# Last transform stage of three batches split into even and odd rows, with sums and differences of index pairs made beforehand

## Chip, cores and metric

One core of one Trainium2 chip. The metric is the device time of one execution in microseconds, the median of several; all runs told of here are fast, with a granted TensorE clock of 0.995 or more. PE is TensorE (PEld its weight loads), DVE VectorE, ACT ScalarE, POOL GpSimd, SP the engine that only issues transfers. A record is one instruction in a trace.

## The reference, cut to what matters

```python
# x, v: (4, 12544, 128)
u = x * v
y = irfft(rfft(u, n=2*S, axis=1) * rfft(h_filt, n=2*S, axis=0)[None], n=2*S, axis=1)[:, :S]   # long convolution
a = (x * y).reshape(4 * 12544, 128)
h = maximum(maximum(a @ w1, a @ w2), a @ w3)                     # 128 -> 768
out = h @ w_out                                                  # 768 -> 128
```

The kernel makes the convolution as a transform of length 128 x 90 with matmuls. The last stage of the inverse goes over 90 indices k1 to 98 rows n: y[n] = sum over k1 of z[k1] * e(n (k1 + 1/4) / 90), real part. Everything is fp32.

## The kernel before

Four batches. Batch 0 is transformed first. Then each of 32 tiles a batch goes through the last transform (`t_last`) and six slots (f = 0 to 5) of the feed-forward part (`up`, `down`), and beside batch b's tiles, slot by slot, the convolution of batch b + 1 runs (`conv_steps`): first its forward part (the u steps), then 45 pairs of k1 (the g steps).

```python
def halves_mm(out, lhsT, rhs, start, stop):        # two 64-column halves, side by side in the array
    for h in range(2):
        nc.tensor.matmul(out[64*h:64*h+64], lhsT[:, 64*h:64*h+64], rhs, ...)

def g_third(b, g):                                  # third transform of a pair of k1, result to DRAM
    ...                                             # 8 matmuls into PSUM ps
    zs = cv.tile([P, 2, 256], tag="z", bufs=2)
    nc.scalar.copy(zs, ps)                          # ACT
    nc.scalar.dma_start(zd[b][2*g:2*g+2], zs)       # issued by ACT

def t_last(i):                                      # last transform of one tile
    for s in range(4):
        for c in range(2):                          # real, imaginary part
            halves_mm(ps[:, s*NB:(s+1)*NB], zt[:, c, s*D:(s+1)*D], f4[:, c, :], ...)   # NB = 98
    nc.vector.tensor_tensor(out=g, in0=ps, in1=xT, op=mult)

def up(i, f):                                       # hps: two PSUM buffers, one for pa, one for pb
    halves_mm(pa, w_sb[1][:, f*P:(f+1)*P], g);  nc.scalar.activation(h, pa, Relu)         # ACT
    halves_mm(pb, w_sb[2][:, f*P:(f+1)*P], g);  nc.vector.tensor_tensor(h, h, pb, max)    # DVE

for f in range(NF):                                 # one slot
    h = up((b, i), f)
    down(*late)                                     # of the slot before
    if f == 3: t_last(tiles[n + 1])
    run(beside.pop(s, ()))                          # this slot's convolution steps
```

`pa` of a slot needs the buffer that ACT's relu of the slot before frees, `pb` the one that DVE's maximum frees. In the views `ops` is the PSUM buffer of `down`, `hid` what relu and maximum write, `eo`, `xt`, `xs` and `ab` are tiles of the g steps, and the first matmuls of the filter's transform (`ps<-f1h`) are called the first quad.

## Time and profile before

| | before |
|---|---|
| time | 2530.8 us (2528.8 to 2533.3) |
| start of the first last transform | 320.7 us |
| batch 0's tiles (batch 1's transform beside) | 581.3 us |
| batch 1's, batch 2's tiles | 586.2, 586.2 us |
| batch 3's tiles (nothing beside) | 452.9 us |
| PE busy | 99% |

The stages run from the first matmul into tile yps of a batch to that of the next (or to the end). The lines that carry the argument are in the prediction.

### The profile page before, as it was taken

The numbers are of one execution on the slowest core, as the hardware profiler recorded it, in microseconds if no ns is written. First come the engines' busy times: TensorE is split into PE (matmuls) and PEld (weight loads), VectorE is DVE, ScalarE is ACT, GpSimd is POOL, SyncE is SP. The second block draws the span as 40 slices with busy tenths as digits, with TensorE's granted clock in tenths as the row PEclk, the third lists the DMA queues.
The fourth block names the chain that finished last, engine by engine and source line by source line (L and its number), as shares of the span: only waits on it lengthen the run. The fifth ranks groups of instructions, "written<-read, shape, count | busy, mean of one in ns | idle before, by whom it ended". The sixth has DMA issues, their size and how long they took to land. (4 is left out here: it accounts for less than half of the span.)

```text
span 2527.3 us, 62508 instructions
## 1 busy us (share of the span) xinstructions
PE 2491.1 (99%) x26393; PEld 1512.2 (60%) x26393; DVE 1259.7 (50%) x2494; ACT 1042.2 (41%) x1980; POOL 57.5 (2%) x112
## 2 busy tenths in 40 slices
PE   8999999999999999999999999999999999999999
PEld 7888755655556556656566556555666654444444
DVE  5588733356666633336666633335667642222222
ACT  2688823344444423334444433333544432222222
POOL 1022200000000000000000000000000000000000
PEclk9999999999999999999999999999999999999999
DMA  7789754477877544466888834447888842222221
GB/s 165 172 251 279 234 122 95 101 179 202 222 208 208 159 104 102 89 143 180 229 222 236 218 91 97 101 105 181 222 234 219 233 112 54 58 59 53 59 53 35
DMA packets 429070, 384.51 MB, mean 152 GB/s; under 512 B 291454, under 2 KB 338293, under 8 KB 428789
## 3 DMA queue, kind: packets, MB, share of 16 engines
q1 hardware_dynamic: 305840, 291.63, 46.1%
q10 hardware_dynamic: 117893, 74.73, 10.3%
q0 software_dynamic: 5056, 14.16, 1.9%
q8 instruction: 206, 3.38, 0.6%
q14 instruction: 75, 0.61, 0.1%
HBM read 295.73 MB, written 84.67 MB: 151 GB/s over the span
## 5 line engine op out<-in xcount | busy, mean ns | idle before, releaser
L473 DVE TENSOR_TENSOR hid<-hid,pb 128x392 f32<-128x392 f32 x768 | 431.8, 562 | 777.6 <-PE pb L126 672.8
L470 ACT ACTIVATE hid<-pa 128x392 f32<-128x392 f32 x768 | 382.2, 498 | 725.2 <-PE pa L126 657.8
L126 PE MATMUL pa<-gt,w_sb 128*64 128x392 f32 x3072 | 640.3, 495 | 11.4 <-ACT hid L470 10.7
L126 PE MATMUL pb<-gt,w_sb 128*64 128x392 f32 x3072 | 636.4, 493 | 4.9 <-DVE hid L473 4.3
L126 PE MATMUL ops<-hid,wo_sb 128*64 128x392 f32 x3072 | 635.8, 492 | 0.1
L126 PEld LDWEIGHTS pb<-gt,w_sb 128*64 128x64 f32 x3072 | 216.6, 136 | 297.4 <-issue 202.4
L126 PEld LDWEIGHTS ops<-hid,wo_sb 128*64 128x64 f32 x3072 | 219.9, 137 | 286.0 <-issue 285.3
L126 PEld LDWEIGHTS pa<-gt,w_sb 128*64 128x64 f32 x3072 | 192.8, 137 | 151.2 <-issue 105.6
L135 PEld LDWEIGHTS ps<-f,uT 98*64 98x64 f32 x4096 | 183.4, 138 | 59.9 <-issue 57.2
L126 PEld LDWEIGHTS yps<-f,zt 90*64 90x64 f32 x4096 | 188.6, 136 | 47.2 <-issue 44.6
L378 DVE TENSOR_TENSOR xt<-xt,ht 128x512 f32<-128x512 f32 x180 | 124.5, 692 | 179.6 <-ACT xs L373 149.4
L126 PEld LDWEIGHTS ps<-ab,wt 128*64 128x64 f32 x2880 | 166.5, 137 | 51.8 <-issue 33.2
L135 PE MATMUL ps<-f,uT 98*64 98x90 f32 x4096 | 195.2, 243 | 1.4 <-issue 1.4
L126 PE MATMUL yps<-f,zt 90*64 90x98 f32 x4096 | 195.3, 247 | 0.0
L401 ACT COPY zs<-ps 128x512 f32<-128x512 f32 x180 | 105.6, 587 | 217.1 <-PE ps L126 211.9
L126 PE MATMUL ps<-ab,wt 128*64 128x128 f32 x2880 | 189.6, 274 | 0.6 <-DVE ab L389 0.6
L126 PE MATMUL ps<-spec,wt 128*64 128x128 f32 x2880 | 187.9, 273 | 0.0
L126 PEld LDWEIGHTS ps<-spec,wt 128*64 128x64 f32 x2880 | 164.6, 137 | 14.9 <-issue 14.7
L461 DVE TENSOR_TENSOR gt<-yps,xT 128x392 f32<-128x392 f32 x128 | 72.5, 567 | 161.0 <-PE yps L126 132.7
L372 ACT ACTIVATE xs<-xt 64x512 f32<-64x512 f32 x180 | 113.1, 628 | 77.4 <-DVE xt L152 46.1
L139 ACT COPY spec<-ps 128x360 f32<-128x360 f32 (+1 forms) x132 | 71.4, 544 | 167.1 <-PE ps L135 167.0
L389 DVE TENSOR_TENSOR ab<-xt 128x256 f32<-128x256 f32 x360 | 136.0, 419 | 1.6
(67 smaller groups left out, 1572.6 us busy)
## 6 DMA issues: line engine op xcount, KB each, us to landing
wt<-wt_const SPq DMA_DIRECT2D x135, 512.0 KB, 4.5
ht<-hd SPq DMA_DIRECT2D x270, 256.0 KB, 5.7
zd<-zs ACTq DMA_DIRECT2D x180, 256.0 KB, 4.8
zt<-zd SPq DMA_DIRECT2D x128, 360.0 KB, 5.7
ut<-in_xr_dram SPq DMA_DIRECT2D x128, 196.0 KB, 3.7
ut<-in_vr_dram SPq DMA_DIRECT2D x128, 196.0 KB, 4.1
xT<-in_x_dram SPq DMA_DIRECT2D x512, 49.0 KB, 4.1
out_dram<-ot ACTq DMA_DIRECT2D x128, 196.0 KB, 3.8
```

The costliest lines, as they stand in the source:

```text
L126: nc.tensor.matmul(out[64 * h:64 * h + 64], lhsT[:, 64 * h:64 * h + 64], rhs, start=start, stop=stop, skip_group_check=True)
L135: nc.tensor.matmul(ps[64 * c:64 * c + 64, 256 * i + r * N1:256 * i + (r + 1) * N1], a[:, r, :], table[:, c * N1:(c + 1) * N1], start=(i % ...
L139: copy(dst, ps[:].rearrange("p (s m) -> p s m", m=256)[:, :, 0:2 * N1].rearrange("p s (r k) -> p k r s", r=2))
L372: nc.scalar.mul(xs[0:64], xt[64:128], -1.0)
L378: nc.vector.tensor_tensor(out=xt[:], in0=xt[:], in1=hts[g][:, 0], op=ALU.mult)
L389: nc.vector.tensor_tensor(out=ab[:, :, q, :], in0=y[:, :, 0, :], in1=y[:, :, 1, :], op=op)
L401: nc.scalar.copy(zs[:].rearrange("p k f -> p (k f)"), ps[:])
L461: nc.vector.tensor_tensor(out=g[:], in0=ps[:, 0:N], in1=xTs.pop(i)[:].rearrange("d p n -> d (p n)"), op=ALU.mult)
L470: nc.scalar.activation(h[:], pa[:, 0:N], Relu)
L473: nc.vector.tensor_tensor(out=h[:], in0=h[:], in1=pb[:, 0:N], op=ALU.max)
```

## The change

For k1 and k1 + 45 the factor e(n k1 / 90) differs by (-1)^n. So even rows n need only sums z[k1] + z[k1 + 45], odd rows only differences. If sums and differences are made before, one pass over 45 real and 45 imaginary parts (again 90 rows of the array) yields the 49 even rows, a second one the 49 odd rows: half the moving columns. The sums are made in `g_third`, as the pair (k1, k1 + 45) is now one step g. The prologue and the folding of the weights were rearranged in the same change.

```diff
-    k1, n = np.arange(N1), np.arange(NB)
+    k1 = np.arange(N1).reshape(2, N1 // 2).T.ravel()      # 0, 45, 1, 46, ...
+    f4p = f4[::2].transpose(1, 0, 2).reshape(N1, NB // 2, 2).transpose(0, 2, 1)
 ...
 def g_third(b, g):
-        nc.scalar.copy(zs[:].rearrange("p k f -> p (k f)"), ps[:])
+        if b == 0:
+            nc.scalar.copy(zs[:].rearrange("p k f -> p (k f)"), ps[:])
+        else:
+            z1 = state["cv"][0].tile([P, 256], FP32, tag="z1", name="z1", bufs=2)
+            nc.scalar.copy(z1[:], ps[:, 256:512])
+            for a, op in enumerate((ALU.add, ALU.subtract)):
+                nc.vector.tensor_tensor(out=zs[:, a], in0=ps[:, 0:256], in1=z1[:], op=op)
         nc.scalar.dma_start(zd[b][2 * g:2 * g + 2]..., zs[:])
 ...
 def t_last(i):                      # batches 1 to 3
+            for s in range(4):
+                for a in range(2):
+                    halves_mm(y[:, s, a * h:a * h + h], zt[:, a, s * D:(s + 1) * D],
+                              f4p[:, a, :], s == 0 and a == 0, True)          # h = 49
 ...
 # prologue: win, eye, back loaded by GpSimd, not ACT
-    warm_up()                        # 16 rounds
+    warm_up(12)
+    window_back()                    # was after the second step of the filter
+    warm_up(20)
 ...
 # folding of the weights: the transpose one step ahead of the product
-    for f in range(NF):
-        folded = fold(f)
-        ...
-        folded()
+    folded = [fold(0)]
+    ...
+    for f in range(1, NF):
+        folded.append(fold(f))
+        folded.pop(0)()
+    folded.pop()()
```

Cut from the diff: two transfers for zt in place of one, the strided view of y, and `signs()`, split off from `window_back`.

More of the change, by code (lines that the diff above doesn't have):

```diff
@@ L40, in tables @@
     S = P * N1
-    k1, n = np.arange(N1), np.arange(NB)
+    k1 = np.arange(N1).reshape(2, N1 // 2).T.ravel()
+    n = np.arange(NB)
     a = e(np.outer(n, k1 + 0.25) / N1)
@@ L62, in tables @@
     f32 = np.float32
-    return f1.astype(f32), f1h.astype(f32), f4.astype(f32), np.ascontiguousarray(both, f32)
+    return f1.astype(f32), f1h.astype(f32), f4.astype(f32), f4p.astype(f32), np.ascontiguousarray(both, f32)
 @with_exitstack
@@ L98 @@
     zd = [dram.tile([N1, 2, 64, 256], FP32, name=f"zd{b}") for b in range(B)]
-    f1_t, f1h_t, f4_t, w_t = tables(NB)
+    f1_t, f1h_t, f4_t, f4p_t, w_t = tables(NB)
     f1_d = nc.inline_tensor(f1_t, name="f1_const").ap()
@@ L103 @@
     f4_d = nc.inline_tensor(f4_t, name="f4_const").ap()
+    f4p_d = nc.inline_tensor(np.ascontiguousarray(f4p_t), name="f4p_const").ap()
     wt_d = nc.inline_tensor(w_t, name="wt_const").ap()
@@ L249 @@
     for h in range(2):
+        nc.gpsimd.dma_start(
+            win[64 * h:64 * h + HH],
+            window[0, h * HH * P:(h + 1) * HH * P].rearrange("(n p) -> n p", p=P))
+    nc.gpsimd.dma_start(eye[:], eye_d)
+    nc.gpsimd.dma_start(back[:].rearrange("p r t -> p (r t)"), back_d)
+    for h in range(2):
         nc.scalar.dma_start(w1_sb[64 * h:64 * h + 64], w1[:, :])
@@ L256 @@
                 posT[:, (h * HH + lo_) * P:(h * HH + hi_) * P])
-    for h in range(2):
-        nc.scalar.dma_start(
-            win[64 * h:64 * h + HH],
-            window[0, h * HH * P:(h + 1) * HH * P].rearrange("(n p) -> n p", p=P))
-    nc.scalar.dma_start(eye[:], eye_d)
-    nc.scalar.dma_start(back[:].rearrange("p r t -> p (r t)"), back_d)
     nc.scalar.dma_start(f1h[:], f1h_d)
@@ L267, with warm_up @@
     nc.scalar.dma_start(f4[:], f4_d)
-    def warm_up():
+    def warm_up(n):
         ps = fps.tile([P, 1024], FP32, tag="cv", name="pw", bufs=2)
-        for _ in range(16):
+        for _ in range(n):
             halves_mm(ps[:, 0:256], warm[:, 0:P], warm[:], True, True)
@@ L281, in window_back, with signs @@
         nc.scalar.copy(winr[:].rearrange("n r t -> n (r t)"), pw[0:64 + HH, 512:512 + P])
+    def signs():
         for sg, lo_, m in ((0, 0, 1.0), (0, FO, 1.0), (1, 0, -1.0), (1, FO, 1.0)):
@@ L444, in t_load @@
         zt = hp.tile([N1, 2, 512], FP32, tag="zt", name="zt", bufs=2)
-        nc.sync.dma_start(
-            zt[:], zd[b][:, :, 2 * i:2 * i + 2, :].rearrange("k c t f -> k c (t f)"))
+        if b == 0:
+            nc.sync.dma_start(
+                zt[:], zd[b][:, :, 2 * i:2 * i + 2, :].rearrange("k c t f -> k c (t f)"))
+        else:
+            for c in range(2):
+                nc.sync.dma_start(
+                    zt[NK * c:NK * c + NK],
+                    zd[b].rearrange("(g a) c t f -> g a c t f", a=2)[
+                        :, :, c, 2 * i:2 * i + 2, :].rearrange("g a t f -> g a (t f)"))
         zts[b, i] = zt
@@ L455, in t_last @@
         ps = yps.tile([D, 512], FP32, tag="y", name="yps")
-        for s in range(4):
-            for c in range(2):
-                halves_mm(ps[:, s * NB:(s + 1) * NB], zt[:, c, s * D:(s + 1) * D],
-                          f4[:, c, :], s == 0 and c == 0, c == 1)
-        g = hp.tile([D, N], FP32, tag="g", name="gt", bufs=2)
-        nc.vector.tensor_tensor(out=g[:], in0=ps[:, 0:N],
-                                in1=xTs.pop(i)[:].rearrange("d p n -> d (p n)"), op=ALU.mult)
+        g = hp.tile([D, 4, NB], FP32, tag="g", name="gt", bufs=2)
+        y = ps[:, 0:N].rearrange("d (p n) -> d p n", p=4)
+        if i[0] == 0:
+            for s in range(4):
+                for c in range(2):
+                    halves_mm(y[:, s, :], zt[:, c, s * D:(s + 1) * D], f4[:, c, :],
+                              s == 0 and c == 0, c == 1)
+        else:
+            h = NB // 2
+            for s in range(4):
+                for a in range(2):
+                    halves_mm(y[:, s, a * h:a * h + h], zt[:, a, s * D:(s + 1) * D],
+                              f4p[:, a, :], s == 0 and a == 0, True)
+            y = y.rearrange("d p (a m) -> d p m a", a=2)
+        xT = xTs.pop(i)
+        if i[0] == 0:
+            nc.vector.tensor_tensor(out=g[:], in0=y, in1=xT[:], op=ALU.mult)
+        else:
+            nc.vector.tensor_tensor(out=g[:].rearrange("d p (m a) -> d p m a", a=2), in0=y,
+                                    in1=xT[:].rearrange("d p (m a) -> d p m a", a=2),
+                                    op=ALU.mult)
         gs[i] = g
     def up(i, f):
-        rhs = gs[i][:]
+        rhs = gs[i][:].rearrange("d p n -> d (p n)")
         h = hp.tile([P, N], FP32, tag="hid", name="hid")
@@ L478, in down @@
             pos_[i] = ops.tile([D, 512], FP32, tag="ops", name="ops")
-            halves_mm(pos_[i][:, 0:N], lin[:], gs[i][:], True, False)
+            halves_mm(pos_[i][:, 0:N], lin[:], gs[i][:].rearrange("d p n -> d (p n)"), True,
+                      False)
         halves_mm(pos_[i][:, 0:N], wo_sb[:, f, :], h[:], False, f == NF - 1)
@@ L534 @@
             mlp_in(i)
-        if i == 1:
-            window_back()
         if i:
             mlp_out(i - 1)
+    signs()
     mps.close()
@@ L658 @@
                 u_first(2 * (s - NK) + v // 2, v % 2, nc.scalar.copy)
-    for f in range(NF):
-        folded = fold(f)
-        if f == 0:
-            u_turn(4)
-            u_turn(5)
-        folded()
+    folded = [fold(0)]
+    u_turn(4)
+    u_turn(5)
+    for f in range(1, NF):
+        folded.append(fold(f))
+        folded.pop(0)()
+    folded.pop()()
     nc.scalar.copy(lin[:], pl[:, 0:D])
@@ L672 @@
     hp = ctx.enter_context(tc.tile_pool(name="hp", bufs=3))
+    f4p = hp.tile([N1, 2, NB // 2], FP32, name="f4p", bufs=1)
+    nc.scalar.dma_start(f4p[:], f4p_d)
     op_ = ctx.enter_context(tc.tile_pool(name="op", bufs=2))
```

## The prediction

> **What bounds the kernel now.** I read the page first (busy shares), then the groups by line, the chain of waits in time, the timeline of one tile, and last the PE waits and the first 60 us.
>
> ```profile
> PE 2491.1 (99%) x26393; PEld 1512.2 (60%) x26393; DVE 1259.7 (50%) x2494; ACT 1042.2 (41%) x1980; POOL 57.5 (2%) x112
> ...
> L126 PE MATMUL yps<-f,zt 90*64 90x98 f32 x4096 | 195.3, 247 | 0.0
> ...
> L401 ACT COPY zs<-ps 128x512 f32<-128x512 f32 x180 | 105.6, 587 | 217.1 <-PE ps L126 211.9
> ```
>
> PE is busy 99% of the span; DVE and ACT have half of it free. The last transform (tile yps) is 4096 records over 128 tiles, 32 a tile. A record's mean of 247 ns is mostly latency, so the cost of a tile is read from start to start, in the chain of waits in order of time (start, length, what) late in batch 3:
>
> ```profile
> 2130.03 1.36 PE yps L126 x32
> 2131.39 0.66 PE pa L126 x4
> 2132.05 0.66 PE pb L126 x4
> ```
>
> One tile's last transform holds PE for 1.36 us (16 pairs of records: two 64-column halves side by side), and the next work starts at once: no wait at either end. A dense group is 4 records (2 pairs) in 0.66 us. So a pair of 98 columns takes 1.355/16 = 84.7 ns (1.355 from the timeline below), a pair of 392 columns 329 ns: near 2 x columns / 2.4 GHz plus 2 to 3 ns (81.7 and 326.7 without the addition). Here the moving columns set the pace. The timeline shows what the weight loads do meanwhile:
>
> ```profile
> 2407.20 1.53 PE L126 MATMUL yps<-f,zt 90*64 90x98 f32 x32
> 2407.20 1.33 PEld L126 LDWEIGHTS yps<-f,zt 90*64 90x64 f32 x30 [0.18 <-issue]
> 2408.47 0.23 PEld L126 LDWEIGHTS pa<-gt,w_sb 128*64 128x64 f32 x4
> 2408.55 0.83 PE L126 MATMUL pa<-gt,w_sb 128*64 128x392 f32 x4
> ```
>
> Each record has its own weight load, which runs under the matmul before it. How long a load holds its path is seen where PE had stood still and two loads follow each other:
>
> ```profile
> 22.92 0.26 PEld L279 LDWEIGHTS pw<-back,winT 128*105 128x105 f32 x2 [0.51 <-ACT winT L278]
> ...
> 707.29 0.20 PEld L126 LDWEIGHTS pa<-gt,w_sb 128*64 128x64 f32 x4 [1.05 <-ACT hid L470]
> ```
>
> In the second line two pairs of 64-column loads end after 0.197 us while one load lasts 0.136: the second pair began about 0.055 us after the first (single records of the trace: 707.287 and 707.342). In the first, 105 columns: 0.26 - 0.17 = 0.09 us. That is 0.86 ns a column, and 54 to 55 ns for 64.
>
> **What the Trainium skill says.** (1) "TensorE: Matmul & The Clock Gate", section "LDWEIGHTS (loading the stationary operand)": a load takes its columns / 1.2 GHz, whatever the rows: 53.3 ns for 64. The trace agrees (55 ns, 90 ns for 105). (2) The same page, "Back-to-back issue gap": in a stream of loads and matmuls the spacing is set by both, and tiny matmuls have a floor of about 25 ns each. With two records side by side that floor would be 50 ns a pair, close to the load's 55; no run here reaches below it. (3) "TensorEngine Tiling (Array Packing)", "Key Properties": different tiles of the array load and multiply in parallel. The trace agrees: the halves start 6 to 8 ns apart. (4) The first page's Part 1 on the clock gate: half clock after an idle window, full clock after some 3.4 us of work. The trace agrees: see the first 23 us below.
>
> **The change part by part.**
>
> *Last transform, 96 of 128 tiles.* The count of matmuls and loads stays (4 positions x 2 x 2 halves); each now moves 49 columns in place of 98. By columns alone a pair would need 2 x 49 / 2.4 + 2 = 43 ns. But each pair still has a 64-column load, 54 to 55 ns, which starts only when the matmul before has begun (about 2 ns after, in the trace). So the load sets the pace: 56.5 ns. Saved per tile: 16 x (84.7 - 56.5) = 451 ns. All of it is on the path, as PE is the bound: 96 x 0.451 = **43.3 us**. So the columns halve, the time falls by a third.
>
> *Sums and differences of k1 and k1 + 45.* In 135 steps (3 x 45) the copy of 128x512 on ACT (587 ns) becomes a copy of 128x256 (373 ns, as the eo copies of the same shape): ACT loses 135 x 0.214 = 29 us. DVE gains 270 operations of the butterfly's form (128x256, one operand in PSUM, 416 ns): 112 us, so 54% of the span in place of 50. None of this is on PE. But DVE works in order: at such a step it stands until PE has ended and ACT has copied. PE needs the maximum (hid) of a step only after the next pa: 0.66 (ops) + the transform work of the slot (about 1.1) + 0.66 us, so most of it is hidden. I allow 4 us for new waits, a choice (30 ns a step).
>
> *Loads and the multiply by x.* zt comes in two transfers of 180 KB, with pieces of the same 2 KB; a tile ahead, so hidden. The product gt reads PSUM with a stride; 0.57 us, possibly more, and needed only three slots (about 6 us) later. Nothing.
>
> *Prologue.* Before, PE and ACT did this (windows of PE: busy, granted clock; timeline):
>
> ```profile
> 17.00:18.00 1.00, 1.00 (x24) 0.50 0.71 199
> ...
> 20.00:21.00 1.00, 1.00 (x34) 1.00 0.85 190
> ```
> ```profile
> 16.10 0.39 ACTq L263 DMA_DIRECT2D f1h<-f1h_const  x1
> ...
> 18.31 1.04 ACTq L267 DMA_DIRECT2D f<-f_const  x1
> 19.39 1.28 ACT L278 ACT_TABLE_LOAD   x1 [19.39 <-DMA w_in<-in_w_dram]
> ...
> 33.37 1.29 DVE L302 SCALAR_TENSOR_TENSOR spec<-pm,winr 105x512 f32<-105x512 f32 x2 [1.03 <-PE pm L294]
> 35.70 1.29 DVE L302 SCALAR_TENSOR_TENSOR spec<-pm,winr 105x512 f32<-105x512 f32 x2 [1.04 <-PE pm L294]
> ```
>
> The filter's first matmuls (pm) started at 16.3 us, when the last piece of pos had landed, partly at half clock, and stood from 22.3 to 25.1 for the window. The change puts the window's matmul ahead of them, and 20 warming rounds between. The window's matmul needs a copy on ACT, and ACT first has to issue its loads. In the new order its fifth constant (f4) takes the place that f1h had, and waits for the same semaphore, so it is issued at about 16.1 us; the table load follows to about 18, copy and matmul to about 18.7. Then 20 rounds of 4 records: 40 pairs of 256 columns at 215 ns warm = 8.6 us, and about 2 us more for a cold start (427 ns a pair at half clock, for some 5 us). So pm would start near 29.5 us in place of 16.3, then run warm: 8 steps of 2.325 us (the period of the two DVE lines) = 18.6, to 48; before, they ended at 40.3. **+7.5 us**, and PE has only about 1.5 us idle in each of the stretches 60 to 110 and 110 to 260 us to take it up. The folding of the weights (PE waited 2.1 us there for ACT, and the matmuls' latency is exposed besides) is now a step ahead: **-2.5 us**.
>
> *Sum:* 2531 - 43.3 + 4 + 7.5 - 2.5 = 2496.7, **2497 us**, 1.3% faster.
>
> **The rivals.** (A) *Loads hide, columns set the pace*: 43 ns a pair, 16 x 41.7 = 667 ns a tile, 64 us; time 2476. For it: loads hide in every 90- and 98-column group. Against it: none of those has a load longer than its matmul, and the 55 ns between two loads was measured with no matmul in the way. (B) *Loads cost more beside short matmuls*: the pm steps above, 64 moving columns, take 2.325 us for 32 pairs, 72.7 ns, where columns alone give 55. If 49 columns ran at that pace, a tile saves 192 ns and the change 18 us: time 2522. Against it: these loads read weights 512 bytes apart, and last 164 ns each where the yps loads last 136, as contiguous ones do everywhere. I take pm as proof that loads set the pace when they are the longer, not for its size. (C) *DVE becomes the gate in the transform stages*: the waits of PE now are
>
> ```profile
> PE pa L126 <- ACT hid L470: 10.7, 30, 0.4
> ...
> PE pb L126 <- DVE hid L473: 4.3, 14, 0.5
> PE ps L126 <- DVE ab L389: 0.6, 1, 0.6
> ```
>
> Small, so there is slack, but the first two are the ones that a stalled DVE lengthens. At 0.2 us for each of 135 steps it would cost 27 us: time 2520. Against it: the three batches' transforms are spread over 172 slots each, about 3 us a slot. (D) *The prologue is no slower*: if ACT reaches the window's copy before pos has landed, the warm start gains some 4 us in place of losing 7.5: time 2485.
>
> **Range and chances.** A, and D with a load of 54 ns, reach below 2480.4 (2% faster); I give them together 1 in 10. B and C lie between 2510 and 2525, together about 1 in 6. Middle 2497, range 2481 to 2514. Slower by 2% would need DVE to hold PE for half a microsecond in each of some 200 steps beyond all gains: 1 in 50.
>
> **What would show each step.** Right: in the chain of batch 3 yps takes 0.90 us for 32 records in place of 1.36, and its stretch from one tile to the next falls from 13.87 to 13.42 us; PEld between yps loads without gaps. A shows as 0.69, B as 1.16. C: PE waits for hid or ab of over 10 us more, in the stretches before 2050 us only, and none in batch 3. Prologue: pm starting near 29 us and the first quad (ps from f1h) near 50 in place of 41.9. The prediction fails if yps is far from 0.90 us, or if the waits for DVE in the transform stages grow past 15 us.

## The result, and the profile after

The changed kernel takes **2551.5 us** (2550.0 to 2555.3) against 2530.8: 0.8% slower. Ratios are the mean time of one kernel's fast runs over that of the other's of the same rounds, so not quite the ratio of the medians quoted; here 1.0084, interval 1.0066 to 1.0101. Forecast was 2497.

The chain of waits in order of time, in batch 3 of the changed kernel (start, length, what):

```profile
2124.51 0.92 PE yps L131 x32
2125.43 0.67 PE pa L131 x4
2126.10 0.66 PE pb L131 x4
```

The last transform fell from 1.36 to 0.92 us, as predicted (0.90). From the page of the changed kernel, the engines' line and two groups:

```profile
PE 2472.6 (97%) x26457; PEld 1470.5 (58%) x26457; DVE 1352.2 (53%) x2764; ACT 1007.4 (39%) x1980; POOL 60.0 (2%) x116
...
L414 DVE TENSOR_TENSOR zs<-ps,z 128x256 f32<-128x256 f32 x270 | 102.1, 420 | 144.5 <-ACT z L412 137.2
...
L412 ACT COPY z<-ps 128x256 f32<-128x256 f32 x135 | 50.3, 373 | 200.9 <-PE ps L131 200.9
```

Durations are as predicted too (420 and 373 ns). New is the last part of the DVE line: before its 270 operations DVE stood for 144.5 us, mostly for ACT's copy. PE's share fell to 97%, and its waits (us in total, times, longest) name who held it:

```profile
PE pa L131 <- ACT hid L505: 36.6, 59, 1.0
PE pb L131 <- DVE hid L508: 19.9, 48, 0.7
```

Before, these were 10.7 and 4.3 us. Where in time:

| stage | before | after |
|---|---|---|
| start of the first last transform | 320.7 | 326.9 |
| batch 0's tiles | 581.3 | 594.7 |
| batch 1's | 586.2 | 594.7 |
| batch 2's | 586.2 | 594.6 |
| batch 3's | 452.9 | 439.7 |

Batch 3 gained its 13 us. Within batch 1, the tiles beside the u steps are 0.4 to 0.5 us shorter each; those beside the g steps are 0.1 to 1.5 us longer. Batch 0's tiles, whose own last transform is unchanged, lost 13 us. So the loss goes with the step that makes the sums. Two instances from the timeline of the changed kernel (start, length, engine; in brackets the idle time before and its releaser). The first:

```profile
1260.15 0.83 PE L131 MATMUL pa<-gt,w_sb 128*64 128x392 f32 x4
...
1260.44 0.37 ACT L412 COPY z<-ps 128x256 f32<-128x256 f32 x1 [0.46 <-PE ps L131]
...
1260.84 0.76 DVE L414 TENSOR_TENSOR zs<-ps,z 128x256 f32<-128x256 f32 x2 [0.72 <-ACT z L412]
...
1261.63 0.37 ACTq L415 DMA_DIRECT2D zd<-zs  x1
1262.04 0.50 ACT L505 ACTIVATE hid<-pa 128x392 f32<-128x392 f32 x1 [1.24 <-PE pb L131]
1262.13 0.83 PE L131 MATMUL ops<-hid,wo_sb 128*64 128x392 f32 x4
...
1262.78 0.83 PE L131 MATMUL pa<-gt,w_sb 128*64 128x392 f32 x4
...
1263.17 0.41 DVE L157 TENSOR_TENSOR xt<-eo,ps 128x256 f32<-128x256 f32 x1
1263.50 0.56 DVE L508 TENSOR_TENSOR hid<-hid,pb 128x392 f32<-128x392 f32 x1
...
1264.11 0.88 PE L131 MATMUL pb<-gt,w_sb 128*64 128x392 f32 x4 [0.50 <-DVE hid L508]
```

Read it downwards. DVE stands 0.72 us for ACT's copy. ACT has ended its copy at 1260.81, but next in its queue is the transfer of zs, which now needs DVE's sums: it is issued at 1261.63. Only then comes the relu, whose input pa was ready at about 1260.98 (last record started at 1260.48, 0.49 us long). The profile puts ACT's idle 1.24 us down to PE's pb, the releaser of a buffer; what held the queue was the transfer ahead. The relu is a microsecond late. That costs nothing here: the next pa starts in its turn, 0.65 us after the group before it. DVE's stand does cost: from 1260.84 on DVE works without a pause through the sums and the operations queued behind them, so it comes to the maximum only at 1263.50, and the next pb on PE stands for 0.50 us. In the second instance it is ACT's stand that costs:

```profile
1243.57 0.37 ACT L412 COPY z<-ps 128x256 f32<-128x256 f32 x1 [2.06 <-PE ps L131]
1243.97 0.76 DVE L414 TENSOR_TENSOR zs<-ps,z 128x256 f32<-128x256 f32 x2 [1.87 <-DMA out_dram<-ot]
...
1244.22 0.83 PE L131 MATMUL pa<-gt,w_sb 128*64 128x392 f32 x4
...
1244.76 0.42 ACTq L415 DMA_DIRECT2D zd<-zs  x1
...
1245.23 0.63 ACT L379 ACTIVATE xs<-xt 64x512 f32<-64x512 f32 x1 [1.29 <-DVE zs L414]
...
1246.78 0.50 ACT L505 ACTIVATE hid<-pa 128x392 f32<-128x392 f32 x1
...
1247.33 0.88 PE L131 MATMUL pa<-gt,w_sb 128*64 128x392 f32 x4 [0.96 <-ACT hid L505]
```

ACT's copy ends at 1243.94, the transfer behind it is issued 0.82 us later, at 1244.76. Everything after it in ACT's queue is late with it, the relu too, whose input was ready at 1245.05 and which starts at 1246.78; PE stands 0.96 us before the next pa. (The profile puts DVE's stand down to a transfer; its sums start 0.03 us after ACT's copy ends.) So the sums can hold PE in two ways: through DVE's own queue, before pb, and through ACT's queue, before pa.

"TensorE: Matmul & The Clock Gate", Part 1, calls the queues of ACT and DVE strict first-in first-out; the trace agrees. Over all 135 steps, single instructions give: ACT stood 110.7 us before these transfers (median 0.82), where before the change it stood 4.0.

The prologue of the changed kernel, from its timeline:

```profile
17.44 1.28 ACT L283 ACT_TABLE_LOAD   x1 [17.44 <-DMA w_in<-in_w_dram]
...
19.04 0.76 PE L284 MATMUL pw<-back,winT 128*105 128x128 f32 x2 [7.63 <-ACT winT L283]
19.73 10.82 PE L131 MATMUL pw<-warm 128*64 128x256 f32 x80
...
30.47 18.82 PE L301 MATMUL pm<-w_sb,specH 64*41 64x64 f32 x512
...
50.89 5.59 PE L140 MATMUL ps<-f1h,spec 105*64 105x90 f32 x96 [1.60 <-DVE spec L309]
```

PE stood 7.6 us for ACT, then did 20 warming rounds, and the first quad came at 50.9 us in place of 41.9, as predicted (near 50).

### The profile page after: what moved, and what is told of

Read it like the earlier page. It is cut to its first block, busy times and chain, and to the rows that moved or that the text cites. A ratio compares the mean times of both kernels' runs of the same rounds, so it can differ in the third digit from the quotient of the medians.

```text
span 2550.6 us, 63123 instructions
## 1 busy us (share of the span) xinstructions
PE 2472.6 (97%) x26457; PEld 1470.5 (58%) x26457; DVE 1352.2 (53%) x2764; ACT 1007.4 (39%) x1980; POOL 60.0 (2%) x116
## 5 line engine op out<-in xcount | busy, mean ns | idle before, releaser
L131 PE MATMUL pb<-gt,w_sb 128*64 128x392 f32 x3072 | 638.4, 494 | 20.5 <-DVE hid L508 19.9
L414 DVE TENSOR_TENSOR zs<-ps,z 128x256 f32<-128x256 f32 x270 | 102.1, 420 | 144.5 <-ACT z L412 137.2
L412 ACT COPY z<-ps 128x256 f32<-128x256 f32 x135 | 50.3, 373 | 200.9 <-PE ps L131 200.9
L390 DVE TENSOR_TENSOR xt<-xt,xs 128x512 f32<-128x512 f32 x180 | 124.6, 692 | 6.3
L131 PEld LDWEIGHTS yps<-f4p,zt 90*64 90x64 f32 x3072 | 106.1, 138 | 35.6 <-issue 33.4
```

What stands on the lines that cost most here:

```text
L131: nc.tensor.matmul(out[64 * h:64 * h + 64], lhsT[:, 64 * h:64 * h + 64], rhs, start=start, stop=stop, skip_group_check=True)
L390: nc.vector.tensor_tensor(out=xt[:], in0=xt[:], in1=xs[:], op=ALU.add)
L412: nc.scalar.copy(z1[:], ps[:, 256:512])
L414: nc.vector.tensor_tensor(out=zs[:, a], in0=ps[:, 0:256], in1=z1[:], op=op)
```

## The experiments

Theory after the result: the sums lengthen a chain through in-order queues (PE's ps, ACT's copy, DVE's sums, ACT's transfer, ACT's relu, PE's pa; beside it, from DVE's sums to DVE's maximum and PE's pb), and PE, with two PSUM buffers for pa and pb, stands at its end. Rivals: DVE has simply too much work; the shorter last transform itself brings the waits out; PSUM buffers are held too long; the prologue is the loss.

### One part at a time: last_only, sums_only, pro_alone

```diff
 # last_only: kernel before + 49-column t_last, with its two transfers for zt (wrong result on purpose)
-        if b == 0:
+        if True:
             nc.scalar.copy(zs[:].rearrange("p k f -> p (k f)"), ps[:])
 # sums_only: kernel before + sums in g_third; t_last and t_load as before (wrong result on purpose)
-        if i[0] == 0:
+        if True:
             for s in range(4): ...        # 98 columns
 # pro_alone: prologue and folding of the change, all transforms as before (right result)
```

> The kernel before with the last transform of batches 1 to 3 cut to 49 columns and nothing else (zs copied whole, prologue and folding as before; the result is wrong on purpose). If the loss of the change comes from the sums alone, this must give the full gain of the shorter transform: 1.355 us a tile before, 0.92 after, 96 tiles, 42 us, so about 2489 us. If shorter PE work in itself brings out waits for ACT and DVE (they have less time between two maxima), the gain in the three transform stages is less than 14 us for each, and the time is 2500 us or more.

Measured: 2496.1 us against 2532.1, ratio 0.986. Most of the gain is there without the sums; the four stages took 582.1, 576.1, 573.3 and 439.1 us. It falls 6 us short of 42. The first last transform started 1.7 us later (322.4): in the profiled run the granted clock was 0.83 from 310 to 330 us, where it was 0.91 before. In the stage of batch 1 PE stood 2.9 us for weights (tile wt) that it had not waited for before. That the faster PE runs into that load is my reading, not shown: sum_later_pool below has the same short transform and no such wait.

> The kernel before with the sums and differences of batches 1 to 3 made (half copied by ACT, two operations on DVE) and nothing else; the last transform moves 98 columns over what it gets, so the result is wrong on purpose. Theory (the sums alone hold PE up, through waits among ACT, DVE and PE in the pair part of each transform stage): the stages lose what the changed kernel lost there, 13.4 us in batch 0's stage and 8.4 + 13.9 = 22.3 us in each of the other two, together 58 us, so about 2589 us. Rival (the loss needs the shorter last transform as well): 13 us in each stage, about 2570 us or less.

Measured: 2585.8 us, ratio 1.0211: **53.7 us slower** from the sums alone, with stages of 594.6, 607.1, 606.9 and 452.6 us, 54.6 more than before in sum. The rival that needs the shorter transform is out. From its page and from its waits of PE:

```profile
PE 2507.5 (97%) x26393; PEld 1507.4 (58%) x26393; DVE 1351.9 (52%) x2764; ACT 1007.3 (39%) x1980; POOL 57.7 (2%) x112
```
```profile
PE pa L131 <- ACT hid L505: 37.6, 59, 1.3
PE pb L131 <- DVE hid L508: 18.8, 44, 0.6
```

The two waits grew by 26.9 and 14.5 us, 41.4 in all; the span of the profiled run grew by 58.0. Another 16.4 us are in PE's *busy* time, 2507.5 against 2491.1 for the same 26393 instructions. Of these, 2.9 come before the first last transform, which started at 324.1 us in place of 320.7. No sum exists yet at that time; the granted clock was 0.97 against 1.00 from 60 to 110 us and 0.83 against 0.91 from 310 to 330. That is not the doing of the sums, and it is left out of the 54.6. The other 13.5 belong to the stands: four records in a row last 0.83 us, but the next group starts after 0.66, so the first 0.17 us of a stand count as busy, and the group after a stand lasts 0.88. By my estimate from these numbers that is 0.22 us for each of 59 more stands, 13 us. So the waits understate what standing costs, here by a quarter.

> The changed kernel's prologue and folding with the transforms of before (right result). The changed kernel starts its first last transform at 326.9 us in place of 320.7: if that is the prologue's doing, 2531 + 6 = 2537 us. If the prologue's delay is made up later, 2531 us.

Measured: 2538.7 us (2532.4 to 2540.0), ratio 1.0021 (1.0006 to 1.0035, so between 1.5 and 9 us): 6.6 us slower by the medians, the first last transform at 327.3 us. It is the prologue's doing, and nothing makes it up later. The parts add to -36.0 + 53.7 + 6.6 = +24.3; the whole change is +20.7.

### Load or order: sum_later_pool

```diff
 def g_third(b, g):                            # batches 1 to 3
             nc.scalar.copy(z1[:], ps[:, 256:512])
-            (sums on DVE, transfer by ACT)
+            z1s[g] = ps, z1
+            return
+    def g_sum(b, g):                          # the two DVE operations, then
+        nc.gpsimd.dma_start(zd[b][2 * g:2 * g + 2]..., zs[:])
 ...
             at(s + lag[4], g_third, b, g)
+            at(s + lag[4] + 1, g_sum, b, g)   # one slot later
```

> The changed kernel with the sums put one slot later on DVE, when ACT's copy is long done, and their transfer issued by GpSimd. Theory (order: DVE stands for ACT's copy, and ACT stands to issue a transfer that now waits for DVE): most of the 58 us comes back, 2495 to 2510 us. Rival (load: 112 us more work on DVE is simply too much beside the rest): the work is the same, so the time stays above 2540 us.

Measured: 2491.1 us (2487.7 to 2491.2), ratio 0.9834: 60 us less than the changed kernel, a little better than expected. From its page by lines, and its waits of PE:

```profile
L422 DVE TENSOR_TENSOR zs<-ps,z 128x256 f32<-128x256 f32 x270 | 101.1, 416 | 0.0
```
```profile
PE pb L131 <- DVE hid L517: 12.3, 19, 1.2
PE pw L284 <- ACT winT L283: 8.0, 1, 8.0
```

The same 270 operations of the same length, with no idle time before them, and the waits for ACT's hid are gone from the top. DVE is busy for 1342.7 us, as in the changed kernel (1352.2). So load is out: order it is. PSUM is out as well: ps is now held a slot longer, and it does no harm.

### Which of the two stands: zd_pool, sum_later

```diff
 # zd_pool: sums at once, as in the change; only
-        nc.scalar.dma_start(zd[b][2 * g:2 * g + 2]..., zs[:])
+        (nc.scalar if b == 0 else nc.gpsimd).dma_start(zd[b][2 * g:2 * g + 2]..., zs[:])
 # sum_later: as sum_later_pool, but
-        nc.gpsimd.dma_start(zd[b][2 * g:2 * g + 2]..., zs[:])
+        nc.scalar.dma_start(zd[b][2 * g:2 * g + 2]..., zs[:])
```

> The changed kernel with one line altered: batches 1 to 3 have the transfer of zs issued by GpSimd, not by ACT. DVE still makes the sums as soon as ACT has copied. If the loss is that ACT stands with the next relu behind a transfer that now waits for DVE, the waits of PE for ACT's hid (36.6 us) fall to about the 10 us of before and the time to about 2515 us. If the loss is DVE standing for ACT's copy, with the butterfly and the maximum behind it, the time stays at 2540 to 2552 us.

Measured: 2510.1 us, ratio 0.9911. One line gave back 41 us. (It also frees ACT of the issue itself, 0.37 us a time; the next run bounds what that is worth.) From its waits of PE and of DVE:

```profile
PE pb L131 <- DVE hid L508: 27.4, 43, 1.1
```
```profile
DVE zs L414 <- ACT z L412: 145.4, 135, 2.0
```

DVE stands for the copy as long as ever (145 us), PE hardly waits for ACT's hid any more (0.6 us in all), but still 27 us for DVE's: DVE's own way to hold PE is left.

> The changed kernel with the sums one slot later on DVE, the transfer still issued by ACT. If DVE's stand for the copy is the loss, about 2495 us, as with GpSimd issuing (2491). If ACT's stand at the transfer is, it remains: ACT still meets the transfer before DVE has done the sums of that slot, and the time stays above 2530 us.

Measured: 2495.8 us, ratio 0.9854. So the second expectation, that ACT's stand would keep the loss, is wrong. ACT still stands before the transfers, longer than in the changed kernel (199 against 111 us, single instructions), and PE waits for ACT's hid only 2.0 us in all (1.4 before pa, 0.6 before pb). From its waits of PE:

```profile
PE pb L131 <- DVE hid L517: 9.1, 21, 0.6
...
PE pa L131 <- ACT hid L514: 1.4, 5, 0.3
```

ACT's issues of the transfer, with all their stands, thus cost only 5 us once the sums come later (2495.8 against 2491.1). The two stands are not two costs to be added (41 and 56 us, of 60): DVE's comes first and makes ACT's, so moving the sums takes out both ways to hold PE, moving the issue only the second. ACT's stand costs when it falls between pa and its relu. Why it now falls elsewhere (the sums come first in the slot, right after the maximum) I have read in the timeline but not tested.

### The prologue: old_pro, and the gaining parts together: sum_later_pool_op

```diff
 # prologue of before in the changed kernel (old_pro) and in sum_later_pool (sum_later_pool_op)
-    warm_up(12)
-    window_back()
-    warm_up(20)
+    warm_up(16)
 ...                                 # win, eye, back loaded by ACT again
+        if i == 1:
+            window_back()
+            signs()
```

> The changed kernel with the prologue of before (order of loads, warming, place of the window's matmul); folding and the rest as changed. The prologue of the change cost 9.0 us at the first quad (50.9 against 41.9 us), the folding gave back about 3: about 2551 - 9 = 2542 us. If the late start is hidden later, 2551 us.

Measured: 2544.0 us, ratio 1.0048 where the change had 1.0084: 7 to 9 us, as expected.

> Sums one slot later, transfer by GpSimd, prologue of before: the parts that gain, without those that lose. 2491 - 9 = 2482 us if they add, near 2% faster than before.

Measured: 2482.3 us (2481.1 to 2487.2), ratio 0.9806 (0.9791 to 0.982). The parts add.

### What sets the pace of the short transform: full_loads

```diff
 # sum_later_pool with
-                    halves_mm(y[:, s, a * h:a * h + h], zt[:, a, s * D:(s + 1) * D], f4p[:, a, :], ...)
+                    nc.tensor.matmul(y[:, s, a * h:a * h + h], zt[:, a, s * D:(s + 1) * D], f4p[:, a, :], ...)
```

> The sums a slot later and by GpSimd's transfer, with the last transform of batches 1 to 3 done in whole matmuls: one load of 128 columns in place of two of 64 side by side, the same 49 moving columns, half as many instructions (right result). Theory (the weight load sets the pace of the short transform): a record takes the load of 128 columns, 107 to 110 ns, and there are 16 of them a tile: 1.75 us a tile in place of 0.92, and the time grows by 96 x 0.83 = 80 us, to about 2571 us. Rival (columns or a fixed cost of an instruction set it): half the instructions take no longer than before, 0.5 to 0.92 us a tile, 2455 to 2491 us.

Measured: 2597.7 us, 107 us more than sum_later_pool. Groups by line of this run:

```profile
L497 PE MATMUL yps<-f4p,zt 90*128 90x49 f32 x1536 | 190.6, 277 | 0.0
L497 PEld LDWEIGHTS yps<-f4p,zt 90*128 90x128 f32 x1536 | 178.7, 192 | 58.7 <-issue 48.3 <-DMA zt<-zd 6.7 <-DMA xT<-in_x_dram 3.7
```

Half the instructions take nearly twice as long in all: single records follow each other at 111.7 ns, the length of a 128-column load, whatever the 49 columns need. The load sets the pace; a fixed cost per instruction does not. The miss of 27 us is at the ends of a tile: batch 3's stage is 475.6 us against 439.5, 1.13 us a tile, of which 16 x 111.7 ns - 0.92 us = 0.87 is pace. In the trace the first 128-column load starts 0.43 us after the start of the last record of ops, where such records follow at 0.33, and the first load of pa about 0.2 us after the start of the last record of yps. "TensorEngine Tiling (Array Packing)", "Key Properties", says that a change of tiling mode drains the engine; that fits, though no other cause was excluded.

### Another prologue, and a mixed place for the sums: best2, mixed

```diff
 # best2: sum_later_pool with GpSimd's loads, 16 rounds, and
+        if i == 0:
+            window_back()
 # mixed: sum_later_pool_op with
+            if b == 1:
+                g_sum(b, g)         # batch 1: at once
 ...
+            if b > 1:
                 at(s + lag[4] + 1, g_sum, b, g)
```

> The sums a slot later and by GpSimd's transfer; in the prologue the window's loads stay with GpSimd, but there are 16 warming rounds as before, and the window's matmul stands between the first two steps of the filter (right result). With the prologue of before this was 2482 us. The steps of the filter should start at 16.3 us and no longer stand 2.8 us for the window: 2480 us, and no worse than 2484. If GpSimd's loads come late or the filter then runs at half clock for longer, 2484 to 2488 us.

Measured: 2484.0 us, ratio 0.9812: no better than the prologue of before (2482.3). Its first quad did come earlier, at 40.4 us against 43.2 in sum_later_pool_op, but the first last transform did not (320.1 against 319.8). In its profiled run the granted clock was 0.97 from 60 to 110 us and 0.83 from 310 to 330, where sum_later_pool_op had 1.00 in both; by my estimate from these shares that is worth up to 1.5 and 3.4 us, more than was gained. Why it fell in this run is not known.

> Prologue of before, transfers of zs by GpSimd, sums at once in batch 1 and a slot later in batches 2 and 3 (right result). Batch 0's tiles, which batch 1's transform runs beside, took 575.1 us with the sums at once and 582.7 with the sums later; the two stages after it 583 and 570. If each stage depends only on where its own sums stand: 2482 - 6 = 2476 us, over 2% faster than before. If the place in one stage matters to the next: 2482 us or more.

Measured: **2477.9 us** (2475.9 to 2480.6), ratio 0.979 (0.9778 to 0.9802), right result: the best version, faster than both kernels. Its interval overlaps that of sum_later_pool_op, though none of its runs reaches one of that kernel's. Stages: 575.6, 569.9, 569.9, 439.6 us; the gain is in the first, which took 580.3 in sum_later_pool_op. Why batch 1's sums, which are spaced differently (172 / (45 + 0.95 x 26) = 2.47 slots a pair against 2.28 in the later batches, by the kernel's formula), are better made at once stays open.

## Why the prediction was wrong

- **What bounds the kernel; loads set the pace** (right). 56.5 ns a pair was predicted, 0.92 us / 16 = 57.5 measured; full_loads confirms the cause. By itself the part gave 36 us, 43 were predicted.
- **Prologue +7.5, folding -2.5** (right in mechanism, about right in size): +5.0 together predicted, +6.6 measured in pro_alone.
- **Work on DVE and ACT** (right): 420 and 373 ns an operation, 54% against the 53% measured.
- **"I allow 4 us for new waits, a choice (30 ns a step)"** (wrong; this step failed). Measured alone: 53.7 us (54.6 in the stages of the traces), 0.40 us for each of 135 steps, 13 times as much. The step before it was sound as far as it went: DVE would stand, and the maximum has slack. It left out two things. It weighed the slack of a single step, and not that DVE comes to the maximum only after all that is queued behind the stand and the sums (19.9 us of PE waiting in place of 4.3). And it left out the other queue. The transfer of zs was issued by ACT, behind ACT's own copy, so it never waited; with DVE between copy and transfer it waits, and the relu waits behind it. The prediction named the maximum alone as what PE needs; of the new PE waits in sums_only almost two thirds (26.9 of 41.4 us) were for the relu. And counting free time (DVE 50%) said nothing about it: sum_later_pool does the same work with 60 us less.
- **Rival C** had the place right, and its sign came true (41.5 us more of waits for hid in the changed kernel, and none in batch 3), but it was given at most 27 us and, with rival B, one chance in six. A rival that lengthens a cross-engine chain inside every slot, in a kernel that is 99% bound by the engine at the chain's end, deserved more.
- **Rival D** is out: the prologue did lose. **Rivals A and B** are out: 0.92 us, not 0.69 or 1.16.

## What to carry to other kernels

When work moves from one engine to two, walk each queue in program order and ask what stands behind every instruction that now waits for another engine, the issue of a transfer included: it holds an in-order engine like any operation. Put the dependent half where its input is long done (a slot later), and issue the transfer from a queue that has nothing else to do; neither is much code, and here they turned +0.8% into -1.7%, and with the old prologue and the sums placed by stage into -2.1%. And halving the moving columns paid here only down to the length of the weight load (57.5 ns a pair, where the load takes 54 to 55 and the columns alone 43).

## What the Trainium skill lacked or had wrong

- "Trainium Kernel Development and Optimization", "Key Constraints", says that issuing transfers from several engines concurrently only saves the sequencer's issue time. That leaves out the wait before the issue. Here moving one transfer per step from ACT to GpSimd saved 41 us (2551.5 to 2510.1) while the transfers waited for DVE and ACT stood 111 us before them, but only 5 us (2495.8 to 2491.1) with the sums a slot later.
- "TensorE: Matmul & The Clock Gate", "LDWEIGHTS (loading the stationary operand)", says that only the columns matter. The filter's loads of 41 columns with weights 512 bytes apart last 164 ns each, those of 64 contiguous columns 136; the steps with them ran at 72.7 ns a pair, where moving columns give 55 and such a load by columns 34. The stride is the only cause that I see, and not tested.
- The same page, "Back-to-back issue gap", has no rule for two 64-column halves side by side. The runs show per pair: 329 ns for 392 moving columns, 84.7 for 98, 57.5 for 49; the greater of 2 x columns / 2.4 GHz and the load of 64 columns (54 to 55), plus 2 to 4 ns.
- "TensorEngine Tiling (Array Packing)", "Key Properties", gives no cost for the drain at a change of mode: full_loads shows about 0.26 us more a tile than its pace explains (1.13 - 0.87), for two changes; that the drain is its cause is not shown.
